# Loading one value tile of a decode-attention kernel as 64 partitions and eight times 8 partitions

## The chip, the cores and the metric

The kernel runs on one core of a Trainium2 chip. The time is the device time of one execution in microseconds, the median of the runs of one kernel. Runs of a kernel agree here within about 0.3%. A run is compared only with runs of the kernel before on the same chip in the same rounds. A change counts as faster or slower from 2% on.

## The reference, cut to what matters

```python
# A: attention with a cache, one new token, B = 4, H = 32 heads, 8192 keys, head width 128, bf16
q      = layernorm(x) @ wq
scores = einsum("bhqd,bhkd->bhqk", q, k_cache) * 128**-0.5
o      = einsum("bhqk,bhkd->bhqd", softmax(scores), v_cache)
h      = x + o @ wo
# B: a gated MLP on layernorm(h), 512 -> 1792 -> 512
out    = h + (sigmoid(g) * u) @ w_down
```

The two caches hold 537 MB. Each byte is read once, so the kernel is a stream of loads with the arithmetic beside it.

## The kernel before: the parts that matter

Two heads make a tile of 128 partitions x 16384 bf16 (4 MB, one contiguous row of 32 KB a partition). There are 64 key tiles and 64 value tiles. They go through a ring of four slots. SyncE issues every load, in order, and waits for a slot's last reader before it refills the slot.

```python
GS = 8; LAG = 10; NS = 4
ring = SB("ring", [128, NS, TW], BF16)          # TW = 16384
...
def kv_src(t, cache):
    h = 2 * t
    return cache[h // H, h % H:h % H + 2, :, :].rearrange("h (p r) d -> (h p) (r d)", p=64)
...
def load(it):
    kind, t = it
    slot = slot_of.get(it)
    if kind == "wo":        # output weights, 8 pieces of 512 rows of 1 KB, issued between the last value tiles
        ...
    if kind == "v" and t == NT2 - 1:   # the last value tile, in three column slices
        ...
    uses[slot] += 1
    sem, val = s_slot[slot], 16 * uses[slot]
    ...
    return [(lambda e: e.dma_start(dst, src).then_inc(sem, 16), sem, val)]

for it in items:            # ... k63, v58, v59, v60, wo0-1, v61, wo2-4, v62, wo5-7, v63, w_gate, w_up, w_down
    dma_of[it] = [P("sp", fn, (), sem, val) for fn, sem, val in load(it)]
```

TensorE multiplies a value tile when the tile's load has raised its semaphore to the full count:

```python
def pe_pv(s, j0=0, j1=4, piece=None):
    ...
    deps.append(dma_of[it][0 if piece is None else piece])
```

## Time and profile before

| | before |
|---|---|
| median time | 1295.36 us (1295.04 to 1295.38, 3 runs) |
| profiled span | 1293.4 us |
| DMA | 9 tenths busy or more in all but the last slice, 426 GB/s mean |
| PE / VectorE / ScalarE busy | 38% / 49% / 5% |

These are lines of the profile page of the kernel before: in 40 equal slices of the span, the busy tenths and the rate of the DMA engines, then the count of packets.

```profile
DMA  9999999999999999999999999999999999999998
GB/s 405 432 428 433 433 427 433 431 430 434 427 431 432 429 431 432 432 428 433 432 430 429 433 429 431 431 432 431 431 429 432 431 429 434 430 430 431 428 382 322
DMA packets 26069, 551.46 MB, mean 426 GB/s; under 512 B 2340, under 2 KB 8232, under 8 KB 9256
```

The rate stands at about 432 GB/s almost to the end. In the records of single packets, a row of 32 KB takes 1.21 us, back to back, on each of 16 engines: 27 GB/s an engine, and a tile of eight rows an engine takes 9.7 us. Nothing else is near its limit, and a microsecond lost by the loads is a microsecond of the kernel. The page's chain of waits, by engine, says the same:

```profile
DMA 80%; PE 12%; SPq 4%; DVE 3%; issue 0%; ACT 0%
```

Last, the trace records for each transfer sixteen landing marks, one for each engine's share. For tile 61 in the kernel before (us of the span):

```
1239.0 1239.5 1239.6 1239.7 1239.8 1240.0 1240.1 | 1244.4 | 1245.5 1245.6 1245.7 1245.8 1246.3 1247.4 1247.5 1247.8
```

Seven engines lead, nine trail by up to 8.7 us. At the start of the kernel all sixteen marks lie within 0.7 us. The trace has 38 instruction packets of 16 KB on the same engines, and the 34 that can be followed each set one engine back by about 1.5 us (the prediction has 1.4).

### The profile page before, as it was taken

What the parts mean: (1) busy time and instruction counts of PE and PEld (TensorE: products, weight loads), DVE (VectorE), ACT (ScalarE), POOL (GpSimd) and SP (SyncE); (2) the same over time, 40 slices, a digit from 0 to 9 for tenths busy, and PEclk for the clock granted to TensorE, in tenths of its full rate; (3) what the DMA queues carried; (4) which work ended last, traced back from release to release, by engine and by line L of the source; (5) the groups of instructions that cost most, each with busy time, mean ns of one, the idle gap of its engine ahead of it and who ended that gap; (6) DMA issues with size and microseconds to landing.
All of it is one profiled execution on the core that took longest, in us unless ns stands there. A gap on an engine that the chain in (4) does not pass through costs nothing.

```text
span 1293.4 us, 10805 instructions
## 1 busy us (share of the span) xinstructions
PE 494.7 (38%) x4867; PEld 183.3 (14%) x4867; DVE 636.9 (49%) x657; ACT 70.7 (5%) x118; POOL 10.7 (1%) x22
## 2 busy tenths in 40 slices
PE   2443334334234244334334334343343343343436
PEld 1011111111011011111111111011111111111114
DVE  5974644545545544635536545545545446445300
ACT  2010100001010010100101010010100101000010
POOL 3000000000000000000000000000000000000000
PEclk8556566566565565565565666665665655665665
DMA  9999999999999999999999999999999999999998
GB/s 405 432 428 433 433 427 433 431 430 434 427 431 432 429 431 432 432 428 433 432 430 429 433 429 431 431 432 431 431 429 432 431 429 434 430 430 431 428 382 322
DMA packets 26069, 551.46 MB, mean 426 GB/s; under 512 B 2340, under 2 KB 8232, under 8 KB 9256
## 3 DMA queue, kind: packets, MB, share of 16 engines
q1 hardware_dynamic: 26016, 550.78, 99.5%
q8 instruction: 38, 0.62, 0.2%
q14 instruction: 7, 0.06, 0.0%
q10 hardware_dynamic: 8, 0.00, 0.0%
HBM read 550.77 MB, written 0.00 MB: 426 GB/s over the span
## 4 chain that ended last, share of the span: by engine, by line
DMA 80%; PE 12%; SPq 4%; DVE 3%; issue 0%; ACT 0%
DMA ring<-in_A_v_cache_dram 76%; PE PS L441 7%; PE PS L417 4%; SPq L222 2%; DMA ring<-in_A_k_cache_dram 2%; DVE kT L399 2%; SPq L238 1%; DMA ring<-in_A_wq_dram 1%; DMA ring<-in_B_w_down_dram 1%; SPq L230 1%; SPq L258 0%; PE PS L332 0%; DVE Lq L376 0%; DVE ring L349 0%; PE PS L359 0%
## 5 line engine op out<-in xcount | busy, mean ns | idle before, releaser
L399 DVE STREAM_TRANSPOSE kT<-ring 128x1024 uint32<-128x1024 uint32 x512 | 587.9, 1209 | 480.9 <-DMA ring<-in_A_k_cache_dram 480.9
L417 PE MATMUL PS<-kT,Lq 128*32 128x512 bf16 x2048 | 241.3, 619 | 570.1 <-DVE kT L399 447.8
L441 PE MATMUL PS<-ring,PTz 128*32 128x512 bf16 x2048 | 215.6, 566 | 205.3 <-DMA ring<-in_A_v_cache_dram 205.3
L417 PEld LDWEIGHTS PS<-kT,Lq 128*32 128x32 bf16 x2048 | 69.0, 136 | 705.4 <-DVE kT L399 481.6
L441 PEld LDWEIGHTS PS<-ring,PTz 128*32 128x32 bf16 x2048 | 64.9, 128 | 323.2 <-DMA ring<-in_A_v_cache_dram 196.8
L476 ACT ACTIVATE negm<-PS 128x1 f32<-128x1 f32 x16 | 2.7, 171 | 1125.1 <-PE PS L472 1125.1
L502 DVE STREAM_TRANSPOSE Et<-Ep 128x512 bf16<-128x512 bf16 x16 | 11.4, 712 | 97.4 <-ACT Ep L498 97.4
L511 ACT ACTIVATE PTz<-Et 64x512 bf16<-64x512 bf16 x32 | 34.0, 1062 | 12.8 <-DVE Et L502 12.5
L516 DVE TENSOR_SCALAR Zs<-PS,rinv 128x512 f32<-128x512 f32 x16 | 11.6, 723 | 37.6 <-PE PS L441 37.6
L523 PE MATMUL PS<-SelZ,Zs 128*128 128x8 f32 x128 | 17.8, 265 | 0.9 <-DVE Zs L516 0.9
L523 PEld LDWEIGHTS PS<-SelZ,Zs 128*128 128x128 f32 x128 | 16.3, 200 | 9.9 <-issue 8.1
L455 DVE TENSOR_REDUCE mx<-PS 128x1 f32<-128x512 f32 x16 | 10.5, 657 | 3.9 <-PE PS L417 3.9
L478 ACT ACTIVATE E_sb<-PS,negm 128x512 bf16<-128x512 f32 x16 | 11.0, 688 | 0.7 <-ACT negm L476 0.2
L498 ACT ACTIVATE Ep<-PS 128x512 bf16<-128x512 f32 x16 | 9.6, 597 | 11.3 <-PE PS L494 11.3
L483 PEld LDWEIGHTS PS<-sig,Gsum 128*128 128x128 f32 x32 | 8.0, 313 | 13.4 <-issue 13.4
L483 PE MATMUL PS<-sig,Gsum 128*128 128x1 f32 x32 | 9.4, 363 | 0.0
L472 PEld LDWEIGHTS PS<-onesf,rowx 1*128 1x128 f32 x32 | 6.8, 265 | 12.5 <-issue 12.5
L472 PE MATMUL PS<-onesf,rowx 1*128 1x1 f32 x32 | 8.2, 323 | 0.0
L494 PE MATMUL PS<-E_sb,Sel 128*32 128x512 bf16 x64 | 7.0, 429 | 1.9 <-ACT E_sb L478 1.3
L349 DVE CAST ring<-PS 128x512 bf16<-128x512 f32 x4 | 2.5, 684 | 9.8 <-PE PS L332 9.8
L528 DVE CAST OT<-PS 128x8 bf16<-128x8 f32 x16 | 2.1, 132 | 9.6 <-PE PS L523 9.6
L332 PE MATMUL PS<-ring,xnT 128*32 128x512 bf16 x32 | 3.5, 615 | 6.6 <-DMA ring<-in_A_wq_dram 6.6
(80 smaller groups left out, 85.4 us busy)
## 6 DMA issues: line engine op xcount, KB each, us to landing
ring<-in_A_k_cache_dram SPq DMA_DIRECT2D x64, 4096.0 KB, 29.7
ring<-in_A_v_cache_dram SPq DMA_DIRECT2D x63, 4096.0 KB, 33.9
ring<-in_A_wq_dram SPq DMA_DIRECT2D x1, 4096.0 KB, 12.3
kT<-in_A_wo_dram SPq DMA_DIRECT2D x8, 512.0 KB, 17.3
ring<-in_A_v_cache_dram SPq DMA_DIRECT2D x1, 2048.0 KB, 18.6
ring<-in_A_v_cache_dram SPq DMA_DIRECT2D x2, 1024.0 KB, 18.2
ring<-in_B_w_gate_dram SPq DMA_DIRECT2D x1, 1792.0 KB, 20.0
ring<-in_B_w_up_dram SPq DMA_DIRECT2D x1, 1792.0 KB, 23.5
```

The source lines that it names most:

```text
L222: return [(lambda e: e.dma_start(wo_v[:, HW * t:HW * t + HW, :], A_wo.rearrange("(h p) f -> p h f", p=128)[:, HW * t:HW * t + HW, :]).then ...
L230: return e.dma_start(ringv(slot)[:, c0:c1], kv_src(t, A_v_cache)[:, c0:c1]).then_inc(s_piece[i], 16)
L238: return e.dma_start(wd_v[:, t0:t1, :], B_w_down.rearrange("(t p) f -> p t f", p=128)[:, t0:t1, :]).then_inc(s_piece[3 + i], 16)
L399: return e.transpose(kT[:, buf, i * q:(i + 1) * q].bitcast(U32), ringv(src)[:, base + i * q:base + (i + 1) * q].bitcast(U32))
L417: mm = e.matmul(bS[g % 2][32 * j:32 * (j + 1), :], Lq[:, l0:l0 + 32], rhs, start=(s % GS == 0 and v == 0), stop=(s % GS == GS - 1 and v == 3),
L441: mm = e.matmul(bO[g % 2][32 * rq:32 * (rq + 1), :], PTz[:, g % 2, l0:l0 + 32], ringv(slot)[:, r0 * 128:(r0 + 4) * 128], start=(s % GS == ...
L472: p2_of[g] = P("pe", lambda e: e.matmul(bX[:, 0:1], rowx[0:1, :], onesf[0:1, 0:1], start=True, stop=True), [d2b_of[g], c_ones])
L483: L_of[g] = P("pe", lambda e: e.matmul(bX[:, 0:1], Gsum[:, :], sig[:, 0:1], start=True, stop=True), [exp_of[g], a1_of[g], d_g])
L502: et_of[g] = P("dve", lambda e: e.transpose(Et[:, :], Ep[:, :]), [epc_of[g]] + list(ptc_of.get(g - 1, ())))
L511: return e.activation(dst, src, ACT.Copy)
L516: z_of[g] = P("dve", lambda e: e.tensor_scalar(Zs[:, :], bO[g % 2][:, :], rinv[:, g % 2:g % 2 + 1], None, op0=ALU.mult), [pv_of[g * GS + G ...
L523: mm = e.matmul(bX[:, 256:264], Zs[:, 128 * r:128 * (r + 1)], SelZ[:, r, :], start=(r == 0), stop=(r == 3))
```

## The change

The intent that the names suggest is to move part of one tile from the trailing engines to "low" engines, which a transfer of 8 partitions is confined to. The bytes, the destination and the semaphore stay the same; TensorE now waits for all nine transfers.

```diff
+        LOW8 = ("v", NT2 - 3)
+        LOW8_PARTS = [(0, 64)] + [(p, p + 8) for p in range(64, 128, 8)]
+
         def load(it):
             kind, t = it
             slot = slot_of.get(it)
+            if it == LOW8:
+                uses[slot] += len(LOW8_PARTS)
+                ops = []
+                for p0, p1 in LOW8_PARTS:
+                    def f(e, p0=p0, p1=p1, sem=s_slot[slot]):
+                        return e.dma_start(ring[p0:p1, slot, :], kv_src(t, A_v_cache)[p0:p1, :]).then_inc(sem, 16)
+                    ops.append((f, s_slot[slot], 16 * uses[slot]))
+                return ops
```

NT2 is 64, so this is value tile 61.

## The prediction

> **What bounds the kernel now.** DMA. The slices of the page show DMA at 9 tenths or more from end to end, at about 430 GB/s. The chain of waits is 80% DMA. The packets of the trace are 32 KB rows that take 1.21 us each, back to back, on 16 engines: 27 GB/s an engine.
>
> The sixteen landing marks of each transfer show that the engines do not keep step. A tile's first engines land 7 to 8.7 us before its last, and this lead grew from 0.7 us at the start. The trace shows 38 instruction packets of 16 KB. Those that can be followed each set one engine back by about 1.4 us, and they fall on eight engines in turn. So about eight engines lead and eight trail. In the tail (timeline) the issuing queue is blocked for 12 and 10 us on output-weight loads, the leading engines run dry around 1243 to 1248 us (about 1 us an engine on average), and the last piece of the down weights lands over 1286 to 1290 us.
>
> **What the change does.** Only the load of value tile 61 changes. By the Trainium skill, "DMA: Bandwidth & Descriptors", section "Why a DMA increments its semaphore by 16 and not by 1", a transfer of 8 partitions uses the 8 lowest-numbered engines alone. No run here shows it yet. So low engines carry 4+8 rows instead of 8, high engines 4: +4.9 us for the low, -4.9 us for the high (4 rows x 1.21 us). If the low ones lead (I think 80%: the instruction packets mostly hit engines that started their first packet late), this levels the tail. At best it recovers about 2 us.
>
> **The cost I expect.** By "SBUF — State Buffer", section "Door 1: The DMA port swizzle", four neighbouring partitions share one port of about 27 GB/s; this trace has only full-width loads and cannot show it. Then 64 partitions reach 8 ports, and 8 neighbouring ones only 2. Four engines share each port, so a block of 256 KB takes up to 4.9 us rather than 1.2. In lockstep the eight blocks would take 39 us; engines that drift apart escape part of it. My estimate for the slowest low engine is 25 to 30 us against 9.7 unobstructed. It would finish tile 61 near 1263 us of the span rather than 1239 (leading engines) or 1248 (trailing). From there it has about 43 us of its own share left, so the end moves from 1290 to about 1303 to 1310 us. The nine issues hide in the blocked queue.
>
> **Prediction:** 1308 us (about +1%), 80% range 1293 to 1322. Faster by over 2%: 1%; within 2%: 86%; slower by over 2%: 13%.
>
> **What the profile would show.** Right: tile 61's small transfers with rows taking 2 to 5 us instead of 1.21; its last landing 12 us or more later than 1248 us; GB/s well under 430 in the slices after about 1235 us; the issuing queue blocked longer; the last down-weights landing 10 to 20 us later, with one group of engines done early. Wrong: rows of the small transfers at 1.21 us; then the tail is levelled, and the time is 1293 to 1296 us.
>
> **What would make it wrong.** Ports that take more than one engine's rate (about 1294). The low engines being the trailing ones (+5 us with free ports, over 1315 with shared). Full lockstep, or a queue that blocks harder on nine transfers and starves the high engines (1320 or more).

## More of the kernel before

The timeline of TensorE shows when each of the last value tiles is first multiplied, and in brackets how long TensorE had been idle, and for what. Columns: start us, length us, engine, line, operation. The lines shown start with tiles 60, 61 and 62:

```profile
1235.08 3.54 PE L441 MATMUL PS<-ring,PTz 128*32 128x512 bf16 x32 [4.64 <-DMA ring<-in_A_v_cache_dram]
1247.81 3.60 PE L441 MATMUL PS<-ring,PTz 128*32 128x512 bf16 x32 [8.21 <-DMA ring<-in_A_v_cache_dram]
1261.91 3.60 PE L441 MATMUL PS<-ring,PTz 128*32 128x512 bf16 x32 [10.51 <-DMA ring<-in_A_v_cache_dram]
```

TensorE waits for each tile, so these starts are landing times.

For three stretches of the tail, the windows view gives the length, the busy time of each engine, the granted TensorE clock, the busy share of the DMA engines and their rate (last column, GB/s):

```profile
1226.00:1240.00 14.00, 8.96 (x76) 4.01 (x68) 1.58 (x4) 5.16 (x8) 0.00 (x0) 0.56 1.01 405
1240.00:1262.00 22.00, 3.69 (x36) 1.17 (x40) 0.00 (x0) 0.00 (x0) 0.00 (x0) 0.62 0.96 370
1262.00:1276.00 14.00, 10.01 (x184) 5.07 (x184) 0.00 (x0) 0.00 (x0) 0.00 (x0) 0.62 1.02 412
```

## The result, and the profile after

| | before | after |
|---|---|---|
| median time | 1295.37 us (1295.04 to 1295.50, 4 runs) | 1323.93 us (1323.65 to 1325.66, 4 runs) |
| ratio, 95% interval | | 1.0224 (1.0206 to 1.0241), slower |
| profiled span | 1293.4 us | 1321.6 us |

The four runs of the kernel before are the three of the first table and one more. A ratio is the mean time of one kernel's fast runs over that of the other's of the same rounds, so it is not quite the ratio of the medians. The change costs 28.6 us, 1.9 us over the top of the predicted range.

The page of the changed kernel, the same three lines:

```profile
DMA  9999999999999999999999999999999999999987
GB/s 409 429 428 431 433 434 429 430 432 431 433 429 432 431 431 429 433 430 432 432 429 431 431 431 433 428 431 434 430 432 427 432 433 434 428 429 431 235 231 303
DMA packets 26133, 551.46 MB, mean 417 GB/s; under 512 B 2404, under 2 KB 8296, under 8 KB 9320
```

The busy digits hardly change, but the rate falls to about half in slices 38 and 39. Busy engines that move half as much are engines that wait for something inside their transfers. The packets under 512 bytes grew by 64: eight small transfers with eight completion packets each, where a transfer on all engines writes sixteen. By the Trainium skill, "DMA: Bandwidth & Descriptors", section "Why a DMA increments its semaphore by 16 and not by 1", a transfer of 8 partitions runs on the lowest 8 engines. The 64 packets agree with eight; the trace does not number the engines.

TensorE's timeline after, again the starts of tiles 60, 61 and 62:

```profile
1240.24 3.59 PE L453 MATMUL PS<-ring,PTz 128*32 128x512 bf16 x32 [9.84 <-DMA ring<-in_A_v_cache_dram]
1276.59 3.60 PE L453 MATMUL PS<-ring,PTz 128*32 128x512 bf16 x32 [31.78 <-DMA ring<-in_A_v_cache_dram]
1290.58 3.61 PE L453 MATMUL PS<-ring,PTz 128*32 128x512 bf16 x32 [10.38 <-DMA ring<-in_A_v_cache_dram]
```

Tile 61 is used 28.8 us later (1276.59 against 1247.81), and tile 62 28.7 us later. From tile 61's start to the end of the span it is 45.0 us after and 45.6 us before. So all of the loss lies ahead of tile 61's landing. Tile 60, whose load was not touched, comes 5.2 us late as well. The windows view after, for the same stretches:

```profile
1226.00:1240.00 14.00, 4.40 (x40) 1.57 (x28) 1.41 (x3) 5.16 (x8) 0.00 (x0) 0.62 1.04 254
1240.00:1262.00 22.00, 4.58 (x40) 2.25 (x40) 0.17 (x1) 0.00 (x0) 0.00 (x0) 0.58 0.90 154
1262.00:1276.00 14.00, 0.00 (x0) 0.00 (x0) 0.00 (x0) 0.00 (x0) 0.00 (x0) 0.50 1.04 237
```

The DMA share stays between 0.90 and 1.04 while the rate is 154 to 254 GB/s. In the packet records, the 50 rows of 32 KB that start between 1229.3 and 1240 us take 2.44 us on average (1.22 us in the kernel before), the 123 that start between 1240 and 1272 us take 2.66 us, up to 3.8. None of the 50 took less than 2.15 us, although some engines were still at tile 60, loaded at full width, until its last mark at 1240.1 us. So the slow rows are not those of the narrow transfers alone; e12 returns to this.

### The profile page after: what moved, and what is told of

Its sections match the earlier page's. It is cut to its first block, busy times and chain, and to the rows that moved or that the text cites. A ratio compares the mean times of both kernels' runs of the same rounds, so it can differ in the third digit from the quotient of the medians.

```text
span 1321.6 us, 10813 instructions
## 1 busy us (share of the span) xinstructions
PE 494.0 (37%) x4867; PEld 183.2 (14%) x4867; DVE 636.9 (48%) x657; ACT 70.7 (5%) x118; POOL 10.6 (1%) x22
## 4 chain that ended last, share of the span: by engine, by line
DMA 79%; PE 11%; SPq 7%; DVE 3%; issue 0%; ACT 0%
DMA ring<-in_A_v_cache_dram 75%; PE PS L453 7%; SPq L234 4%; PE PS L429 4%; DMA ring<-in_A_k_cache_dram 2%; DVE kT L411 2%; SPq L250 1%; DMA ring<-in_A_wq_dram 1%; SPq L230 1%; DMA ring<-in_B_w_down_dram 1%; PE PS L344 0%; DVE Lq L388 0%; SPq L242 0%; SPq L270 0%; DVE ring L361 0%
```

## The experiments

**Theory A (ports).** By the Trainium skill, "SBUF — State Buffer", section "Door 1: The DMA port swizzle", four neighbouring partitions share one port of 27 GB/s, and 64 partitions of one half reach only 8 of the 16 ports. Then the first half of the tile runs at half rate, eight engines meet at two ports in each small transfer, and engines that serve other tiles on those ports slow down too. **Theory B (load).** The low engines carry twelve rows in place of eight, and that, with two of them possibly trailing, is the cost. **Theory C (count).** Nine transfers cost by their number. **Theory D (tail).** The issuing queue, blocked by the output weights, adds a second wait.

All times are medians; "before" is that of the same rounds; the last column is when TensorE starts on tile 61 in the profiled run. By the 2% rule e2 to e6 and e9 to e11 count as the same as before. Except for e2, their intervals still lie clear of 1, and where the text below draws on a difference between two variants, the ranges of their runs do not overlap. The rounds were on several chips; the kernel before took 1295.14 to 1295.51 us in them.

| run | us | before | ratio (95%) | tile 61 starts |
|---|---|---|---|---|
| the change | 1323.93 | 1295.37 | 1.0224 (1.0206 to 1.0241) | 1276.59 |
| e1 probe | 1295.33 | 1295.42 | one run | |
| e2 nine column slices | 1295.63 | 1295.42 | 1.0001 (0.9986 to 1.0016) | 1247.97 |
| e3 two halves | 1310.94 | 1295.42 | 1.0120 (1.0105 to 1.0135) | 1264.43 |
| e4 spread, upper half | 1315.65 | 1295.42 | 1.0162 (1.0145 to 1.0179) | 1268.43 |
| e5 spread, lower half | 1309.05 | 1295.22 | 1.0106 (1.0090 to 1.0123) | 1261.83 |
| e6 load moved, no neighbours | 1304.38 | 1295.22 | 1.0070 (1.0055 to 1.0085) | 1256.28 |
| e7 change at tile 30 | 1324.23 | 1295.22 | 1.0221 (1.0206 to 1.0236) | |
| e8 output weights on ScalarE's queue | 1348.02 | 1295.22 | 1.0411 (1.0395 to 1.0426) | 1279.92 |
| e9 as e6, neighbours | 1309.80 | 1295.14 | 1.0111 (1.0095 to 1.0126) | 1261.62 |
| e10 as e6, every eighth | 1309.26 | 1295.14 | 1.0111 (1.0095 to 1.0128) | 1261.71 |
| e11 neighbours, even load | 1307.38 | 1295.14 | 1.0095 (1.0080 to 1.0110) | 1261.60 |
| e12 change at tile 1 | 1332.62 | 1295.51 | 1.0283 (1.0266 to 1.0301) | |

In every variant of tile 61 on SyncE's queue alone, the start of tile 61 moves by what the time moves, within 1.6 us: 16.6 us for 15.5 in e3, 8.5 for 9.2 in e6, 28.8 for 28.6 in the change. All of these runs gave correct results.

### e1: which engines carry a transfer of 8 partitions

```diff
+        if it in PROBES:     # behind value tiles 20, 40, 58
+            P("sp", lambda e: e.dma_start(probe[:, n, :], kv_src(0, A_k_cache)[0:8, 0:64]).then_inc(s_probe, 16), ...)
```

> The kernel before, and behind the loads of value tiles 20, 40 and 58 a load of 8 partitions x 128 bytes each into a scratch tile that nothing reads. If such a load runs on 8 engines only, it has 8 landing marks from data (and the 8 others at once). Theory A (the prediction's: the low 8 engines lead): for tile 58 the 8 marks come with the tile's first 7 or 8 marks, 6 us or more before its last. Theory B (the low 8 trail, formed from the trace after): the 8 marks come with the tile's last 8 or 9 marks. Time within 0.2% of before either way.

The marks of value tile 58 and of the probe behind it (the probe's eight other increments came at once, when it was issued):

```
tile 58: 1207.27 1207.36 1207.42 1207.52 1207.59 1207.72 1208.22 | 1212.33 | 1213.58 1213.59 1213.64 1213.67 1213.73 1213.75 1213.93 1215.50
probe:   1207.59 1207.70 1207.76 1207.93 1208.41 | 1212.51 | 1213.84 1213.94
```

Neither theory held whole. The transfer does run on eight engines. Five of them lead, one is in the middle, and two are among the trailing eight. The probes behind tiles 20 and 40 split in the same way, five and three (behind tile 40, marks at 857.9 to 858.6 and at 861.9 to 862.6 us). A tile is done when its last engine is done, so a transfer to the low engines starts, for its landing, with those two.

### e2: nine transfers, all of full width

```diff
-        LOW8_PARTS = [(0, 64)] + [(p, p + 8) for p in range(64, 128, 8)]
+        LOW8_PARTS = [(0, 8192)] + [(c, c + 1024) for c in range(8192, 16384, 1024)]   # columns of all 128 partitions
```

> Tile 61 again in nine transfers, one of half the bytes and eight of 256 KB, but each over all 128 partitions (column slices). Port theory: each transfer reaches all ports and all engines, so 1295 to 1298 us. Overhead theory (nine transfers cost by their number, in issue, queue or completion): near 1320 us.

The time is that of before (1295.63 against 1295.42 us). Nine transfers cost nothing by their number, down to rows of 2 KB. Theory C is out.

### e3: two halves, all engines equally loaded

```diff
+        LOW8_PARTS = [(0, 64), (64, 128)]
```

> Tile 61 in two transfers of 64 partitions, all 16 engines with equal bytes, only two transfers. Port theory: each half reaches half of the ports, rows take about 2.4 us instead of 1.21, the tile costs up to 9.7 us more on every engine: 1302 to 1306 us. Theory that only the uneven load of the low engines matters: 1295 to 1296 us.

TensorE's timeline of e3, the start of tile 61:

```profile
1264.43 3.60 PE L453 MATMUL PS<-ring,PTz 128*32 128x512 bf16 x32 [19.62 <-DMA ring<-in_A_v_cache_dram]
```

Two transfers in place of one, with equal bytes an engine, cost 15.5 us. Load cannot be the reason, and count is out by e2. What each of the two lacks is width. The size was more than expected: half rate for the whole tile would be 9.7 us. Tile 60 is late in e3 too (it starts at 1239.39 us, 4.3 us late), so the half-width transfers also hold up engines that are still at an earlier tile: all 104 rows of 32 KB that start between 1230 and 1250 us take 2.16 us or more. That is a part of the excess; the rest was not followed.

### e4 and e5: the same eight engines, every fourth partition

```diff
+        # e4: LOW8_PARTS = [(0, 64, 1)]   + [(p, p + 29, 4) for h in (64, 96) for p in range(h, h + 4)]
+        # e5: LOW8_PARTS = [(64, 128, 1)] + [(p, p + 29, 4) for h in (0, 32)  for p in range(h, h + 4)]
-        ring[p0:p1, slot, :], kv_src(t, A_v_cache)[p0:p1, :]
+        ring[p0:p1:step, slot, :], kv_src(t, A_v_cache)[p0:p1:step, :]
```

> As the change, but the eight transfers of 8 partitions take every fourth partition (64, 68, ... 92 and so on), so that each reaches eight ports instead of two. Same engines, same bytes an engine, same number of transfers. Port theory: rows of these transfers take 1.2 to 2.4 us, no crowd of four at a port; what is left is the first half (64 partitions) and the double load of the low engines: 1303 to 1310 us. Theory that number of transfers or the load of the low engines makes the 28 us: 1320 to 1325 us.

> The halves' roles swapped against the spread variant: partitions 64 to 127 come in one transfer on all engines, partitions 0 to 63 in eight transfers that each take every fourth partition. If the low engines write partitions 0 to 63 anyway in a full-width load (one engine to a port), then these eight transfers disturb nobody and nobody disturbs them: rows of 1.2 us, and 1303 to 1310 us, 5 to 12 us below the spread variant's 1315.65. If it makes no difference which half the low engines write (their double load alone counts), 1313 to 1318 us.

TensorE's timelines, the start of tile 61, first of e4:

```profile
1268.43 3.61 PE L453 MATMUL PS<-ring,PTz 128*32 128x512 bf16 x32 [23.99 <-DMA ring<-in_A_v_cache_dram]
```

and of e5:

```profile
1261.83 3.61 PE L453 MATMUL PS<-ring,PTz 128*32 128x512 bf16 x32 [15.97 <-DMA ring<-in_A_v_cache_dram]
```

Both keep the change's engines, bytes an engine and number of transfers. Spreading the partitions alone (e4) takes 8.3 us off the change's 28.6. It was less than expected: 1315.65 us lies above the range given for theory A and below that for theory B. Letting the low engines fill partitions 0 to 63 rather than 64 to 127 (e5) takes off 6.6 us more. This agrees with the section "The descriptor swizzle" of "DMA: Bandwidth & Descriptors", by which engines 0 to 7 fill partitions 0 to 63 in every full-width load and the others 64 to 127: in e4 the low engines write where the high ones write their own tiles, in e5 they do not.

### e6: the load moved, without neighbours

```diff
+        LOW8_PARTS = [(0, 128, 1, 0, 8192)] + [(p, p + 29, 4, 8192, 16384)
+                      for h in (0, 32, 64, 96) for p in range(h, h + 4)]     # p0, p1, step, columns
```

> The same 2 MB moved to the low engines with no crowd of neighbours anywhere: half of every row in one full-width transfer, the other half in 16 transfers of 8 spread partitions. If the move of load alone costs what 4 rows take, and two of the low engines trail as the probe showed: about +5 us, 1300 us; up to 1306 us as the low engines meet the high ones at the ports of partitions 64 to 127. If load alone is the main cost of the change: 1315 us or more.

1304.38 us: moving 2 MB to eight engines costs about 9 us even where no neighbours meet. This is theory B's share, at most, as the low engines still write to partitions 64 to 127 beside the high ones.

### e9 and e10: the same with neighbours, and with every eighth partition

```diff
+        # e9:  [(p, p + 8, 1, 8192, 16384)  for p in range(0, 128, 8)]
+        # e10: [(p, p + 57, 8, 8192, 16384) for h in (0, 64) for p in range(h, h + 8)]
```

> As the load-only variant (1304.38 us: half of every row full-width, the other half in 16 transfers of 8 partitions on the low engines), but the 8 partitions of each transfer are neighbours: two ports instead of eight. Same bytes an engine, same count of transfers. Port theory: 1312 to 1322 us, the difference to 1304.38 being the crowd alone. If crowding does not matter and load alone does: 1303 to 1306 us.

> The same with every eighth partition (p, p+8, ... p+56): the partitions are farther apart than in the load-only variant, but by the Trainium skill's port table they meet on four ports, two engines each. Port table: between the two, 1306 to 1314 us, and slower than the load-only variant by 2 us or more. If only nearness in partition number mattered: 1303 to 1306 us.

e9 fell short of its range: the neighbours cost 5.4 us over e6 (1309.80 against 1304.38), not 8 or more. e10 matters more. Its partitions are farther apart than e6's, yet it costs as much as e9's neighbours (1309.26 us). So what counts is not nearness in partition number; a spacing of 4 is better than both 1 and 8. This fits the port table: a spacing of 4 reaches eight ports, a spacing of 8 within a half only four. But e9 reaches two ports and e10 four, and their times do not differ, so the cost is not in proportion to the crowd. Nor do these runs separate the two ends of a transfer: a partition always takes the same row of the cache, so a crowd where the rows are read, and not at the ports, is excluded by no run here.

### e11: neighbours, all sixteen engines, no load moved

```diff
+        LOW8_PARTS = [(0, 128, 1, 0, 8192)] + [(p, p + 16, 1, 8192, 16384) for p in range(0, 128, 16)]
```

> The second half of every row in 8 transfers of 16 neighbouring partitions: all 16 engines carry equal bytes (no load moved), but each transfer meets on four ports. Port theory: 2 MB at a quarter of the ports would take 19 us instead of 4.9, engines that drift apart escape part of it: 1301 to 1310 us. If the load moved to the low engines is the cause: 1295 to 1297 us.

The windows view of e11, for the stretch in which TensorE waits for tile 61:

```profile
1240.00:1262.00 22.00, 0.40 (x4) 0.14 (x8) 0.00 (x0) 0.00 (x0) 0.00 (x0) 0.54 0.92 210
```

Here every engine carries what it carried before, and 12.2 us are lost all the same (1307.38 us), at a DMA share of 0.92 and 210 GB/s where the kernel before has 0.96 and 370. With e3 this is the plainest case against theory B as the main cause.

### e7: the change far from the tail

```diff
-        LOW8 = ("v", NT2 - 3)
+        LOW8 = ("v", 30)
```

> The change made to value tile 30 in place of 61, far from the tail. If the blocked queue of the tail (small-row weight loads waiting between the value tiles) adds to the cost, mid kernel is cheaper by about 7 us: 1312 to 1319 us, since the kernel is DMA-bound there too. If the depth of the buffers absorbs the delay: under 1300 us. If the tail adds nothing: 1322 to 1326 us.

The windows view of the kernel before over the stretch in which e7's loads are slow:

```profile
654.00:697.00 43.00, 14.45 (x139) 4.56 (x135) 19.97 (x20) 3.59 (x6) 0.00 (x0) 0.62 1.00 430
```

and of e7 over this stretch and the one after:

```profile
654.00:697.00 43.00, 1.90 (x16) 0.45 (x16) 9.13 (x8) 0.00 (x0) 0.00 (x0) 0.54 1.00 175
697.00:720.00 23.00, 8.47 (x86) 2.80 (x90) 10.13 (x11) 0.00 (x0) 0.00 (x0) 0.57 0.98 420
```

29.0 us are lost, as in the tail, with no output weights near. The engines are busy all the time (share 1.00) and move 175 GB/s, where the kernel before moves 430 in the same 43 us. So theory D is wrong. In the tail some engines run dry while the queue is blocked; in mid kernel none runs dry, and the loss is the same. That they would otherwise only meet the others at the ports is my reading of it. It also shows that the four buffers regain nothing later, as DMA has no slack.

### e8: the output weights on another queue

```diff
-        for it in items:
-            dma_of[it] = [P("sp", ...)]
+        # all but "wo" on SyncE's queue; the eight "wo" pieces on ScalarE's, after its last softmax work
+        for i in range(NWO):
+            dma_of[("wo", i)] = [P("act", fn, (), sem, val) for fn, sem, val in load(("wo", i))]
```

> The changed kernel with the eight output-weight loads issued on ScalarE's queue, after its last softmax work, so that they no longer stand between the value tiles on SyncE's queue. If the second wait (engines dry around 1244 to 1262 and 1282 to 1290 us because the queue is blocked) is a part of the cost: 1314 to 1320 us. If only the crowded rows count: 1322 to 1325 us.

ScalarE's timeline of e8, the issue of the last five pieces, then TensorE's first use of them:

```profile
1233.00 79.13 ACTq L234 DMA_DIRECT2D kT<-in_A_wo_dram  x5
```

```profile
1323.35 3.56 PE L598 MATMUL PS<-OT,kT 128*128 128x4 bf16 x128 [29.82 <-DMA kT<-in_A_wo_dram]
```

The kernel got 24 us slower still (1348.02 us), outside both ranges. The issue of five pieces took 79 us, and the weights became the last thing to land: TensorE used them at 1323.35 us, where the kernel before used them at 1266.50. In the packet records rows of 1 KB of one queue and rows of 32 KB of the other alternate on the engines (274 small and 173 large ones start between 1240 and 1275 us). This agrees with what "DMA: Bandwidth & Descriptors" says in "Queues, rings and completion order", that an engine goes round its queues packet by packet; a queue of small rows beside one of large rows then gets few bytes. As a test of theory D the run failed, since it brought a new wait; e7 decided that.

### e12: the change where the engines are in step

```diff
-        LOW8 = ("v", NT2 - 3)
+        LOW8 = ("v", 1)
```

> The change made to value tile 1, where the landing marks of the kernel before show the engines within about 2 us of each other (near tile 61: 8.7 us). If the trailing engines' lag is a part of the cost of the change: cheaper than at tiles 30 and 61, 1314 to 1320 us. If engines that are in step crowd the ports longer (eight blocks in lockstep, up to 39 us): 1326 to 1336 us. If neither matters: 1322 to 1325 us.

TensorE's timeline at tile 1, of the kernel before:

```profile
101.99 1.90 PE L441 MATMUL PS<-ring,PTz 128*32 128x512 bf16 x16 [3.17 <-DMA ring<-in_A_v_cache_dram]
```

and of e12:

```profile
141.40 1.90 PE L453 MATMUL PS<-ring,PTz 128*32 128x512 bf16 x16 [40.72 <-DMA ring<-in_A_v_cache_dram]
```

The windows view over the slow stretch, of the kernel before:

```profile
98.00:140.00 42.00, 14.11 (x137) 4.18 (x129) 21.36 (x21) 0.00 (x0) 0.00 (x0) 0.58 1.01 434
```

and of e12:

```profile
98.00:140.00 42.00, 1.90 (x16) 0.44 (x16) 5.23 (x5) 0.00 (x0) 0.00 (x0) 0.50 0.97 117
```

The loss is 37.1 us, the tile comes 39.4 us late, and the engines, busy for 0.97 of these 42 us, move 117 GB/s. 120 rows of 32 KB take over 4 us, 4.75 us on average. That is close to four times 1.21 us, as with four engines at one port. This is the lockstep case that the prediction had named as the worst one (39 us for the eight blocks; here an engine spends 36 to 38 us on them). Engines out of step, as near tile 61, crowd each other less.

But who is slowed does not fit theory A. The eight blocks have only 64 rows. When the packets are followed engine by engine, by the end of one and the start of the next, 59 of the 120 slow rows are rows of blocks, and 61 belong to the eight engines that carry no block and are already at later tiles, loaded at full width. All 85 rows that start between 105 and 132 us take 4.77 to 5.00 us, on all sixteen engines. In e7 the 70 that start between 672 and 688 us take 3.33 to 3.69 us, again on all sixteen. A block reaches two ports, so theory A would slow only a few of the other eight at a time. The ports can account for how slow the rows become; what passes the slowness on to every engine was not tested and stays open.

### No better kernel

No variant beats the kernel before. e2 equals it, all others are slower. Ports give a reason, which was argued and not tested: a row's port is fixed by its destination, so giving it to another engine does not take its bytes from the port, and the ports are as full as the engines.

## Why the prediction was wrong

- **What bounds the kernel, right.** DMA, with nothing hidden. e7 shows that the same loss in mid kernel costs the same.
- **Eight engines for a transfer of 8 partitions, right.** The 64 added completion packets and the probe's eight marks show it.
- **Crowded ports as the main cost, right in effect, the place not shown.** e3, e10, e11 and e12 show that the cost comes with the partitions that a transfer is confined to, at equal loads, at other spacings and in lockstep; rows took 2 to 4 us in the change. That the crowd is at the ports rests on the sizes, two times 1.21 us in the halves and four times in e12's blocks. The prediction also expected one group of engines to be done early; e7 and e12 show all sixteen slowed alike.
- **The failed step: "It would finish tile 61 near 1263 us of the span".** TensorE could start on the tile only at 1276.59 us. Two terms of that sum were wrong. First, by its numbers the sum began with the leading engines, at 1229 us plus 5, on the ground that the low engines lead. The probe shows that five of the eight lead and three come later, at tile 58 by up to 6.4 us. What this did stands in the landing marks of the changed kernel: after 1265 us only twelve marks of tile 61 are left, in groups of about three some 2.5 us apart (1266.1 to 1267.2, 1268.9 to 1269.7, 1271.6 to 1271.9, then 1274.2 twice and 1276.6). So five low engines were done by 1264.7 us, close to 1263, and the tile waited for the other three. In e7, where the packets can be followed engine by engine, five low engines end their blocks at 688.6 to 691.6 us and three at 696.6 to 697.2. Second, the first half was put in at 4.9 us (4 rows x 1.21). The prediction itself says that 64 partitions reach 8 ports, and gave that no cost. The rows of that stretch took 2.44 us, so four rows are 9.8 us, 4.9 us more; e3 shows the effect by itself. With 8.7 us, by which the last of all sixteen engines trails at tile 61, 1263 + 8.7 + 4.9 is 1276.6. That it fits so closely is partly luck, since the low engines' own lag was smaller at tile 58. The start of the trailing low engines was not changed by itself in any run.
- **"25 to 30 us" for the slowest low engine in the eight blocks, about right.** From tile 61's own 9.7 us and the delay of 28.8 us, its engines spent 38.5 us on it; less 9.8 us for the first half, 28.7 us are left for the blocks (worked out, not marked in the trace). In e7 the low engines take 25.5 to 27.9 us for them.
- **"about 43 us of its own share left", right in what it was for.** From the tile's use to the end it is 45.0 us after and 45.6 us before: nothing further is lost.
- **"At best it recovers about 2 us".** No run recovered any. e6, the move without neighbours, lost 9 us.
- **The odds.** A loss over 2% got 13%, and a fully crowded or trailing case was named as the way to it. Part of both was true at once.

## What to carry to other kernels

Where DMA bounds a kernel as it does here, cut a load by columns rather than by partitions: nine column slices cost nothing, and two halves of the partitions cost 15.5 us, for a tile that takes 9.7. Ask not only what a narrow transfer costs the engines that carry it: here it slowed the other engines as much. When an estimate starts from "the engines that lead", ask for the landing of the last engine of the set, since that is what the semaphore waits for. And once a sum names a limit, price every term that falls under it, the plain-looking first transfer too.

## What the Trainium skill lacked or had wrong

- "SBUF — State Buffer" gives the rate of one narrow transfer. It does not say that such a transfer slows the full-width loads beside it: tile 60, untouched, came 5.2 us late, and the whole core fell from 430 to 175 GB/s for 43 us (e7), with all sixteen engines slowed alike. "DMA: Bandwidth & Descriptors" tells of slowness that spreads to other engines only for copies between cores ("Back-pressure in remote DMA").
- "DMA: Bandwidth & Descriptors" says of two transfers to the halves of the partitions that they serialize. In a stream of loads they cost more than that: 15.5 us for a tile of 9.7 us (e3).
- The port count of one transfer, by which "SBUF — State Buffer" orders the rates, did not order the times: two ports (e9, 1309.80 us) and four (e10, 1309.26 us) cost the same, eight (e6, 1304.38 us) less. No page has that engines out of step escape a part of the crowd: 28.6 us lost where the marks lie 8.7 us apart, 37.1 us where they lie about 2 us apart (e12).
- No page has that instruction packets put the engines out of step: landing marks 0.7 us apart at the start, 8.7 us near tile 61, with 38 such packets in the trace.
- "DMA: Bandwidth & Descriptors" says that spreading loads over issuing engines saves only issue time. Small rows on a second queue did worse than that: 79 us to issue five pieces, and 24 us lost (e8).
